# Products of zeros in TensorE's planned gaps before the first tokens, in an attention and two-layer feed-forward kernel

## The chip, the cores and the metric

One Trainium2 chip, one of its cores. The metric is the device time of one execution in microseconds (us), less is better. The engines are TensorE (PE; its weight loads are shown apart as PEld), VectorE (DVE), ScalarE (ACT), GpSimd (POOL) and SyncE (SP), which issues the transfers.

## What is computed

Two attentions over the same q, k, v (4 batches, 8 heads, 576 tokens, 64 per head) are added: one over means of 4 tokens, whose rows are repeated 4 times, and one local, where a token sees those less than 4 places away. The sum goes, as 2304 tokens of 512, through two feed-forward layers.

```python
out_d = sm_attn(q_d, k_d, v_d)            # q_d, k_d, v_d: means over 4 tokens
out_up = np.repeat(out_d, factor, axis=2)
mask = np.abs(pos[:, None] - pos[None, :]) < factor
scores = np.where(mask, scale * np.matmul(q, k.transpose(0, 1, 3, 2)), -1000000000.0)
...
out_local = np.matmul(attn, v)
x = (out_up + out_local)                  # as 2304 x 512
x = ((x @ w_a) * (x @ w_b)) @ w_out       # d_ff 1536
h = x @ w_in                              # d_ff 2048
return (h * np.clip(h + 3.0, 0.0, 6.0) / 6.0) @ w_out2
```

All is float32. The weights arrive as 64-bit numbers and are decoded on the chip.

## The kernel before

The work is cut into steps. Each step is handed to a planner, the class `Plan`, with its engine, the time that it will keep the engine busy, a due time (`want`), the steps that it comes after, and tokens that it takes and gives back (buffers, banks of PSUM, turns). `Plan.run` lets time pass by these costs. Whenever an engine is free, the ready step with the least due time that can have its tokens is begun, and its instructions are written into the program at that moment. So the plan fixes the order of instructions on each engine, once; on the chip each engine runs its instructions in that order and waits for the data of each. The planner's times are in us: 0.07 + 0.00106 n for VectorE over n elements (`dve`), 0.0039 per KB of a transfer plus 2.5 until it has landed, and 0.35, 0.25 and 0.2 from the end of a step of TensorE, ScalarE or VectorE until another engine may use the result.

The 2304 tokens are cut into units of 116 (the last of each batch has 112), and the units into seven blocks: two units in the first, three in the others. The steps that matter here, with their lines:

- `pooled`, once for each batch and pair of heads g: load q and k (L372, 590 KB by the plan's count) and v (L377); sums of 4 tokens on VectorE (L395); scores on TensorE (L405, 2.0 by the plan in the first batch; 32 matrix products of float32 there, 64x72 against 64x144); maximum (L410) and scale (L413) on VectorE; exponentials on ScalarE (L419); normalisation on VectorE (L352); two transposes on TensorE (L437), each followed by a copy on ScalarE (L444); products with v on TensorE (L455); a copy on ScalarE (L461).
- `local`, once for each unit: mask and scores on TensorE (L497, L503); maximum on VectorE (L511); exponentials on ScalarE (L520); normalisation (L352); transposes (L536) and a copy (L540); products with v on TensorE, which in the first batch start from the pooled part (L546, L550); then the tokens x in two float32r parts, the first by ScalarE (L571), the second by VectorE (L574).
- `decode`: each 1024 KB piece of a weight goes through one ScalarE step (L240), eight VectorE instructions (L246 to L271) and one more ScalarE step (L268).
- `job`: for one block and one piece of w_a and w_b, 24 products on TensorE (L609), a copy (L615) and a product (L618). The first job needs the tokens of both units of the first block.

Everything later (L666, the first layer's output; L792 and L915, the second layer by seven products in place of eight) is TensorE's for the most part.

PSUM in this stage has two pairs of banks, token "s2", for scores, and four single banks, token "b", for transposes, for value products and for the jobs' sums. At most one transpose ("turn", 1) and one value product ("pv", 1) hold a bank at a time, and "m" (3) caps the banks that jobs hold. A score of the pooled attention takes a pair that the exponentials give back, so the third score waits for the exponentials of the first.

In the plan the first four scores, those of the four pairs of heads of batch 0, begin at 5.68, 7.98, 10.80 and 16.95 on TensorE.

Of the kernel before, what the change touches and what calls it, by code (L numbers as in the profile page):

```python
# [11 lines left out]
BF16 = mybir.dt.bfloat16  # L12
# [6 lines left out]
P = 128  # L19
# [12 lines left out]
BLOCKS = (2, 3, 3, 3, 3, 3, 3)  # L32
XT = 3 * UT
NC = 512
NB = 384
CUT = 4
BANK = 512
# [19 lines left out]
class Plan:  # L57
# [4 lines left out]

    def __init__(self):
        self.steps, self.cap, self.queue = [], {}, {}
        self.loose = set()

    def add(self, engine, busy, want, run, after=(), take=(), give=(), late=0.0):

        i = len(self.steps)
        self.steps.append((engine, busy, (want, i), run, [a for a in after if a is not None], take, give, late))  # L70
        for tag in take:
            self.queue.setdefault(tag, []).append((want, i))
        return i

    def run(self):
        left = [len(s[4]) for s in self.steps]
        users = [[] for _ in self.steps]
        for i, s in enumerate(self.steps):
            for a in s[4]:
                users[a].append(i)  # L80

        for q in self.queue.values():
            heapq.heapify(q)
        ready, free, events, now, done = {}, {}, [], 0.0, 0
        for i, s in enumerate(self.steps):
            ready.setdefault(s[0], [])
            free[s[0]] = 0.0
            if not left[i]:
                heapq.heappush(ready[s[0]], s[2])

        def can(i):
            return all(self.cap[tag] > 0 and (tag in self.loose or self.queue[tag][0][1] == i)
                       for tag in self.steps[i][5])

        while True:
            moved = True
            while moved:
                moved = False
                for engine, steps in ready.items():
                    if free[engine] > now:  # L100
                        continue
                    for w in sorted(steps):
                        if can(w[1]):
                            break
                    else:
                        continue
                    steps.remove(w)
                    heapq.heapify(steps)
                    i = w[1]
                    _, busy, _, run, _, take, give, late = self.steps[i]  # L110
                    for tag in take:
                        self.cap[tag] -= 1
                        if tag not in self.loose:
                            heapq.heappop(self.queue[tag])
                    run()
                    done += 1
                    moved = True
                    free[engine] = now + busy
                    heapq.heappush(events, (now + busy, -1, i))
                    heapq.heappush(events, (now + busy + late, i, i))  # L120
            if not events:
                break
            now, kind, i = heapq.heappop(events)
            if kind < 0:
                continue
            for tag in self.steps[i][6]:
                self.cap[tag] += 1
            for u in users[i]:
                left[u] -= 1
                if not left[u]:  # L130
                    heapq.heappush(ready[self.steps[u][0]], self.steps[u][2])
        if done != len(self.steps):
            stuck = [(engine, self.steps[i][3].__qualname__.split("fused_kernel")[-1], w, self.steps[i][5], self.cap)
                     for engine, steps in ready.items() for w, i in steps]
            raise RuntimeError(f"{len(self.steps) - done} steps cannot begin, as {stuck[:9]}")
# [3 lines left out]
def fused_kernel(ctx: ExitStack, tc: tile.TileContext, qk, vt, vd, wab, wo, w2i, w2o, mask, out):  # L139
    nc = tc.nc  # L140
# [16 lines left out]
    ap = actx.enter_context(tc.tile_pool(name="attn", bufs=1))  # L157
# [7 lines left out]
    ready = const.tile([P, 1], F32, name="ready")  # L165
# [2 lines left out]
    make_identity(nc, ident)  # L168
    ident16 = ap.tile([P, P], BF16, name="ident16")
    make_identity(nc, ident16)  # L170

    h_d = [dram.tile([P, NT], F32, name=f"h_d{f}") for f in range(F1)]

    plan = Plan()
# [9 lines left out]
    def slot(pool, shape, dtype, tag, name):  # L184
        return pool.tile(shape, dtype, tag=tag, bufs=BUFS[tag], name=name)
# [16 lines left out]
    def PE(busy, want, run, after=(), take=(), give=(), slack=0.0):  # L202
        return plan.add("PE", busy, want, run, after, take, give, PE_L + slack)
# [9 lines left out]
    def DMA(kb, want, run, after=(), take=(), give=()):  # L213
        i = plan.add("SP", dma(kb), want, run, after, take)
        j = plan.add("-", 0, want, lambda: None, [i], give=give, late=DMA_L)
        issued[j] = i
        return j
# [116 lines left out]
    def unit_tokens(u):  # L334
        return min(UT, S - u % NU * UT)

    place, sizes = {}, []
    for m, n in enumerate(BLOCKS):
        sizes.append(0)
        for _ in range(n):  # L340
            u = len(place)
# [6 lines left out]
    S_ = {}  # L348
# [8 lines left out]
    def one_bank(name):  # L357
        return slot(ps, [P, BANK], F32, "b", name)
# [274 lines left out]

    cuts = list(range(0, NT, NC)) + [NT]
    spans = list(zip(cuts, cuts[1:]))
    hs, accs, x2_d = {}, {}, {}

    def hg_slot(f, name):
        return slot(pools["p3" if f % 4 == 3 else "p2"], [P, 2, NC], F32R, f"hg{f % 4 // 3}", name)

# [3 lines left out]
    def second(n, f, want):  # L644
# [45 lines left out]
        for e in range(KC):  # L690
            T = {}

            def out_of(e=e, T=T):
                T["t"] = (slot(pools["p4"], [P, NB], F32, "c", "x2f") if end else
                          slot(pools["p3"], [P, NC], F32, "xo", "x2f"))[:, :nb]
                nc.scalar.activation(T["t"], accs[n][e], AF.Copy)

            def store(e=e, T=T):
                for m in range(lo // NB, (hi - 1) // NB + 1):
                    if m not in x2_d:  # L700
                        x2_d[m] = dram.tile([KC, P, NB], F32, name=f"x2_d{m}")
                    a, b = max(lo, m * NB), min(hi, m * NB + NB)
                    nc.sync.dma_start(x2_d[m][e][:, a - m * NB:b - m * NB], T["t"][:, a - lo:b - lo])

            tag = "c" if end else "xo"
            j = ACT(act(nb), want, out_of, [i, S_["p4"] if end else None], take=[tag], give=["q"])
            j = DMA(nb // 2, want, store, [j], give=[tag])
            for m in range(lo // NB, (hi - 1) // NB + 1):
                S_.setdefault(("x2d", m), []).append(j)
# [270 lines left out]
    for u in place:  # L980
        m = place[u][0]
        i = (place[u][1] + UT - 1) // UT
        t = when[m, 0] - 4 + 0.1 * i if m < 3 else T1 - 30 + 4 * i if m == 3 else T1 - 14 + 1.25 * (i + 3 * m - 12)
        if u % NU == 0:
            for g in range(HP):
                pooled(u // NU, g, t - 0.05 + 0.01 * g, u // NU < 1)
        local(u, t, m < 3 and unit_tokens(u) == UT)
    for f in range(F1):
        S_["wab", f] = decode(wab[f], when[0, f] - 4, lambda f=f: wab_t.setdefault(f, slot(wpool, [P, 2, W], F32R, "wh", "wh")),
                              "wh", ahead=26 if f < 2 else 6, slack=0.0)  # L990
# [118 lines left out]
    for i, (n, h) in enumerate((n, h) for n in ORDER for h in range(2)):  # L1109
# [8 lines left out]
        def second(n=n, h=h):  # L1118
# [4 lines left out]
                take=["wh" if i < F1 else "w2"])  # L1123
        j = ACT(act(W), T4 - 4 + 4 * i, first, [j])
        S_["w2o", n, h] = DVE(dve(W), T4 - 4 + 4 * i, second, [j])
    for p in range(PAIRS):
        outer(p, T4 + 56 * p)
    plan.run()


# [67 lines left out]
```

## Time and profile before

| | us |
|---|---|
| median of 3 runs | 946.65 |
| lowest and highest | 945.78, 947.98 |
| the profiled execution | 948.64 |
| its span, first to last instruction | 946.8 |
| TensorE busy in the span | 927.8 |
| VectorE busy | 756.0 |
| ScalarE busy | 456.3 |

The profile is of one execution. Busy times add up an engine's instructions; a clock of 1.00 means that TensorE is granted its upper level, 2.4 GHz, and 0.50 the lower, 1.2 GHz. Where the profile has no record of the clock (the first stretches) the table shows 1.00. Matrix products overlap: one that takes 294 ns from begin to end can be followed by the next much sooner.

### The profile page before, as it was taken

Reading aid. Unit: us, or ns where it says so; the run is one execution under the profiler, and the core shown is the slowest. Engines: PE = TensorE matmul, PEld = TensorE weight load, DVE = VectorE, ACT = ScalarE, POOL = GpSimd, SP = SyncE. Lnnn points to the kernel's source line nnn. Section 1 sums busy time; section 2 is a strip of 40 time slices with the busy share of each in tenths; the row PEclk is TensorE's granted clock in tenths of the full one; section 3 lists DMA queues with packets and bytes.
Section 4 is the critical chain, followed back from the end, with each engine's and each line's share of the span. In section 5 each row is a group of like instructions: output and inputs, shape, how many; then the busy total and the mean of one; then the engine's idle time right before and its main releaser. Section 6 shows DMA issues by size and latency. Waiting matters only on the chain.

```text
span 946.8 us, 19011 instructions
## 1 busy us (share of the span) xinstructions
PE 927.8 (98%) x7246; PEld 874.9 (92%) x7246; DVE 756.0 (80%) x1375; ACT 456.3 (48%) x1164; POOL 5.4 (1%) x44
## 2 busy tenths in 40 slices
PE   7899999999999999999999999999999999999998
PEld 6678989999989999998888889999999999999998
DVE  4999999924736959686877856999898999897983
ACT  4677455423555424233444435555455574554551
POOL 1000000000000000000000000000000000000000
PEclk9799999999999999999999999999999999999999
DMA  9644563423205444426677887425248871806301
GB/s 272 181 131 151 188 213 136 142 85 117 96 31 158 159 139 142 134 70 201 192 229 249 262 255 234 143 96 189 105 159 266 269 256 53 282 2 212 123 18 52
DMA packets 103726, 151.26 MB, mean 160 GB/s; under 512 B 8785, under 2 KB 72273, under 8 KB 103633
## 3 DMA queue, kind: packets, MB, share of 16 engines
q1 hardware_dynamic: 102944, 148.80, 49.0%
q8 instruction: 57, 0.93, 0.4%
q10 hardware_dynamic: 688, 1.23, 0.4%
q14 instruction: 37, 0.29, 0.1%
HBM read 100.19 MB, written 49.81 MB: 158 GB/s over the span
## 4 chain that ended last, share of the span: by engine, by line
PE 86%; DVE 10%; DMA 1%; issue 1%; ACT 1%; SPq 0%; DVEq 0%; ACTq 0%
PE pab L609 32%; PE ph L792 16%; PE oacc L915 15%; PE acc L666 14%; PE po L550 2%; PE dsc L405 2%; DVE in L722 2%; PE sc L503 1%; PE pt L536 1%; PE dpo L455 1%; DVE w2o L1120 1%; DMA h<-h_d 1%; DVE e L888 1%; DVE part L808 1%; PE po L546 1%
## 5 line engine op out<-in xcount | busy, mean ns | idle before, releaser
L609 PE MATMUL pab<-x,wh 128*128 128x344 f32 (+2 forms) x2016 | 321.3, 318 | 0.1
L609 PEld LDWEIGHTS pab<-x,wh 128*128 128x128 f32 x2016 | 308.0, 189 | 3.6 <-issue 1.9
L915 PE MATMUL oacc<-w2o,in 128*128 128x256 f32 x1512 | 181.9, 283 | 1.4 <-DVE in L722 1.4
L915 PEld LDWEIGHTS oacc<-w2o,in 128*128 128x128 f32 x1512 | 181.3, 192 | 2.0 <-DVE in L722 1.8
L792 PE MATMUL ph<-in,w 128*128 128x384 f32 x1008 | 175.4, 335 | 0.0
L792 PEld LDWEIGHTS ph<-in,w 128*128 128x128 f32 x1008 | 175.2, 188 | 0.0
L666 PE MATMUL acc<-h,wo 128*128 128x512 f32 (+1 forms) x720 | 151.2, 371 | 1.3 <-ACT h L654 0.8
L666 PEld LDWEIGHTS acc<-h,wo 128*128 128x128 f32 x720 | 125.7, 188 | 26.8 <-DVE h L658 1.7
L808 DVE TENSOR_TENSOR part<-ph,part 128x384 f32<-128x384 f32 x168 | 86.1, 554 | 9.3 <-PE ph L792 8.6
L618 DVE TENSOR_TENSOR a<-a,pab 128x344 f32<-128x344 f32 (+2 forms) x84 | 41.4, 494 | 56.3 <-PE pab L609 46.7
L816 ACT ACTIVATE r<-part,three 128x384 f32<-128x384 f32 x96 | 56.4, 613 | 54.9 <-DVE part L808 52.4
L654 ACT ACTIVATE h<-h 128x512 fp32r<-128x512 f32 (+1 forms) x60 | 35.1, 589 | 81.5 <-DMA h<-h_d 63.5
L615 ACT ACTIVATE a<-pab 128x344 f32<-128x344 f32 (+2 forms) x84 | 36.8, 445 | 77.7 <-PE pab L609 53.2
L658 DVE TENSOR_TENSOR h<-h 128x512 fp32r<-128x512 f32 (+1 forms) x60 | 37.9, 636 | 37.4 <-ACT h L654 37.3
L719 ACT ACTIVATE in<-gr 128x384 fp32r<-128x384 f32 x96 | 47.4, 521 | 41.4 <-PE oacc L915 29.0
L240 ACT ACTIVATE m<-raw 128x1024 f32<-128x1024 f32 x34 | 39.3, 1155 | 42.6 <-DVE raw L258 23.4
L722 DVE TENSOR_TENSOR in<-gr,in 128x384 fp32r<-128x384 f32 x96 | 50.2, 563 | 7.0 <-ACT in L719 6.3
L719 ACT ACTIVATE in<-e 128x384 fp32r<-128x384 f32 x72 | 36.5, 526 | 33.9 <-PE oacc L915 21.3
L819 DVE SCALAR_TENSOR_TENSOR r<-r,part 128x384 f32<-128x384 f32 x96 | 50.7, 555 | 1.2 <-ACT r L816 1.1
L520 ACT ACTIVATE e<-sc,mx 128x64 f32<-128x64 f32 x160 | 48.1, 322 | 5.3 <-DVE mx L512 5.3
L258 DVE SCALAR_TENSOR_TENSOR raw<-raw,m 128x1024 f32<-128x1024 uint32 x34 | 41.7, 1227 | 1.2
L251 DVE SCALAR_TENSOR_TENSOR raw<-raw,m 128x1024 uint32<-128x1024 uint32 x34 | 41.5, 1221 | 0.2
(86 smaller groups left out, 899.3 us busy)
## 6 DMA issues: line engine op xcount, KB each, us to landing
g_d<-r SPq DMA_DIRECT2D x96, 192.0 KB, 1.9
gr<-g_d SPq DMA_DIRECT2D x48, 384.0 KB, 4.9
raw<-wab SPq DMA_DIRECT2D x12, 1024.0 KB, 11.2
h<-h_d SPq DMA_DIRECT2D x48, 256.0 KB, 3.1
h_d<-a SPq DMA_DIRECT2D x48, 172.0 KB, 1.9
raw<-w2o SPq DMA_DIRECT2D x32, 256.0 KB, 3.5
qk<-qk SPq DMA_DIRECT2D x14, 576.0 KB, 5.7
w2o<-w_d SPq DMA_DIRECT2D x14, 512.0 KB, 10.1
```

The lines of the kernel that those rows point to most:

```text
L251: nc.vector.scalar_tensor_tensor(out=hi, in0=hi, scalar=0xC0000000, in1=T["m"].bitcast(U32), op0=ALU.bitwise_and, op1=ALU.bitwise_or)
L258: nc.vector.scalar_tensor_tensor(out=lo.bitcast(F32), in0=lo, scalar=2.0 ** -52, in1=m, op0=ALU.mult, op1=ALU.mult)
L520: nc.scalar.activation(L["e"][:, p, h], L["s4"][:, p, h], AF.Exp, bias=L["mx"][:, p, h:h + 1], scale=SCALE, accum_out=L["z"][:, p, h:h + 1])
L609: nc.tensor.matmul(T[k], wab_t[f][:, x, c], xs[n][:, g, y, :nb], start=(g == 0 and i == 0), stop=(g == KC - 1 and i == 2))
L666: nc.tensor.matmul(accs[n][e], wo_t[f // 2][:, x, c], hs[n, f][:, y], start=(f == 0 and i == 0), stop=(f == F1 - 1 and i == 2))
L719: nc.scalar.activation(x[0][:, 0], src(), AF.Copy)
L722: nc.vector.tensor_tensor(x[0][:, 1], src(), x[0][:, 0], op=ALU.subtract)
L792: nc.tensor.matmul(acc[k], t[:, x, g * P:(g + 1) * P], X[k, g][0][:, y], start=(g == 0 and n == 0), stop=(g == 1 and n == 2))
L808: nc.vector.tensor_tensor(s[name], acc[k], s[other], op=ALU.add)
L816: nc.scalar.activation(T["r"], src(), AF.Relu, bias=three)
L819: nc.vector.scalar_tensor_tensor(out=T["r"], in0=T["r"], scalar=6.0, in1=src(), op0=ALU.min, op1=ALU.mult)
L915: nc.tensor.matmul(acc[n][e], X[n, k][0][:, x, e * P:(e + 1) * P], t[:, y], start=(k == 0 and i == 0), stop=(k == K - 1 and i == 2))
```

## The change

The class `Plan` gets a `filler`. When an engine is free and none of its ready steps can begin, and the engine is the filler's, and the time since the last filler is at least 0.4 (`FILL`), the filler is run: it keeps the engine busy for 0.25 in the plan, and two events wake the planner, one at its end and one 0.4 after its beginning. The filler is one product of a 128x128 tile of bf16 zeros with the same tile repeated four times, 512 columns, into a bank that nothing reads. That bank is taken from "b" and counted once in "m" by a first step, due before everything else, which also runs the first such product; a last step, which keeps no engine busy, ends the filling and gives both tokens back when ScalarE has written the first token part of both units of the first block. The zeros are written by one memset on VectorE, behind that of `three`.

```diff
+FILL = 0.4
...
+        self.filler = None
...
-        ready, free, events, now, done = {}, {}, [], 0.0, 0
+        ready, free, events, now, done, fill = {}, {}, [], 0.0, 0, 0.0
...
                     else:
+                        if self.filler and engine == self.filler[0] and now >= fill:
+                            _, busy, period, run = self.filler
+                            run()
+                            free[engine], fill = now + busy, now + period
+                            heapq.heappush(events, (now + busy, -1, -1))
+                            heapq.heappush(events, (fill, -1, -1))
                         continue
...
+    idle = ap.tile([P, P], BF16, name="idle")
+    nc.vector.memset(idle, 0.0)
+    unread = []
+
+    def fill():
+        if not unread:
+            unread.append(one_bank("unread"))
+        nc.tensor.matmul(unread[0], idle, idle.unsqueeze(1).to_broadcast([P, BANK // P, P]), start=True, stop=True)
...
+    def end_fill():
+        plan.filler = None
+
+    i = plan.add("PE", 0.01, -1000, fill, take=["b", "m"])
+    plan.add("-", 0, -1000, end_fill, [i, *(S_["x", u] for u in place if place[u][0] < 1)], give=["b", "m"])
...
+    plan.filler = ("PE", 0.25, FILL, fill)
     plan.run()
```

## Rows read from the trace of the kernel before

**Rows 1.** The page: busy us, share, instructions; granted clock in 40 slices, in tenths.
```profile
PE 927.8 (98%) x7246; PEld 874.9 (92%) x7246; DVE 756.0 (80%) x1375; ACT 456.3 (48%) x1164; POOL 5.4 (1%) x44
...
PEclk9799999999999999999999999999999999999999
```

**Rows 2.** Stretches: begin:end, us, busy of each engine (instructions), clock, DMA share, GB/s.
```profile
12.60:21.27 8.67, 8.51 (x140) 7.66 (x141) 6.18 (x16) 6.42 (x37) 0.00 (x0) 1.00 1.05 272
21.27:39.50 18.23, 14.52 (x230) 11.63 (x229) 17.78 (x30) 13.32 (x55) 0.00 (x0) 0.87 0.78 235
39.50:45.00 5.50, 5.49 (x69) 3.51 (x70) 4.81 (x9) 3.75 (x15) 0.00 (x0) 0.51 0.28 70
45.00:50.80 5.80, 5.67 (x85) 3.79 (x85) 5.51 (x13) 4.89 (x23) 0.00 (x0) 1.00 0.91 276
50.80:66.00 15.20, 14.82 (x204) 12.12 (x203) 14.19 (x33) 8.99 (x38) 0.00 (x0) 1.00 0.35 102
```

**Rows 3.** Waits of VectorE, 21 to 66: us in total, times, longest.
```profile
DVE dmx L410 <- PE dsc L405: 1.4, 1, 1.4
DVE x L574 <- ACT x L571: 0.6, 1, 0.6
DVE a L618 <- PE pab L609: 0.6, 2, 0.3
```

**Rows 4.** Line L405 in 5.5 to 10.5 and 10.8 to 14: ns least/median/most.
```profile
L405 PE MATMUL dsc<-dqk,qk x38: 443/444/524, 5.9 to 10.3; 64*72 64x144 f32 x38
...
L405 PE MATMUL dsc<-dqk,qk x44: 283/294/409, 10.6 to 13.9; 64*72 64x144 f32 x44
```

**Rows 5.** The chain of waits in order of time: start, us, what.
```profile
5.93 4.15 PE dsc L405 x32
```

**Rows 6.** TensorE in order of time, 12 to 16: start, us, line, operation, tiles.
```profile
12.76 2.41 PE L405 MATMUL dsc<-dqk,qk 64*72 64x144 f32 x32 [0.22 <-ACT de L419]
...
15.38 0.39 PE L497 MATMUL sc<-mask_sb,ident 128*128 128x256 bf16 x2
15.70 0.69 PE L503 MATMUL sc<-qk 64*64 64x64 f32 x32
```

**Rows 7.** VectorE in order of time, its first two instructions.
```profile
0.80 0.06 DVE L164 MEMSET three<- 128x1 f32 x1 [0.80 <-PEq L1188]
...
5.12 0.75 DVE L395 TENSOR_REDUCE dqk<-qk 128x144 f32<-128x576 f32 x1 [4.26 <-DMA qk<-qk]
```

**Rows 8.** Groups of instructions on TensorE, 431 to 700: count, busy, mean ns, idle.
```profile
L666 PE MATMUL acc<-h,wo 128*128 128x512 f32 (+1 forms) x720 | 151.2, 371 | 1.3 <-ACT h L654 0.8 <-DVE h L658 0.3
```

**Rows 9.** TensorE in order of time, 39.5 to 47.
```profile
39.51 1.92 PE L546 MATMUL po<-od,ident 128*128 128x464 f32 x2 [0.39 <-ACT od L461]
41.36 1.97 PE L550 MATMUL po<-eT,vz 128*64 128x58 f32 x32
43.26 0.61 PE L497 MATMUL sc<-mask_sb,ident 128*128 128x256 bf16 x2
43.80 1.14 PE L503 MATMUL sc<-qk 64*64 64x64 f32 x32
44.86 1.04 PE L546 MATMUL po<-od,ident 128*128 128x464 f32 x2
45.84 1.15 PE L550 MATMUL po<-eT,vz 128*64 128x58 f32 x32
```

**Rows 10.** One more stretch, with the columns of rows 2.
```profile
123.40:126.80 3.40, 3.40 (x13) 3.40 (x13) 3.33 (x6) 0.32 (x1) 0.00 (x0) 0.50 1.03 374
```

**Rows 11.** TensorE in order of time, just ahead of that stretch.
```profile
122.49 0.72 PE L405 MATMUL dsc<-dqk 64*72 64x144 f32 x8 [1.62 <-DVE dqk L395]
```

**Rows 12.** ScalarE and VectorE in order of time, 42 to 45.
```profile
43.40 0.56 ACT L571 ACTIVATE x<-po 128x464 fp32r<-128x464 f32 x1 [1.75 <-PE po L550]
...
42.15 1.22 DVE L271 TENSOR_TENSOR wh<-raw,wh 128x1024 fp32r<-128x1024 f32 x1
...
43.99 0.64 DVE L574 TENSOR_TENSOR x<-po,x 128x464 fp32r<-128x464 f32 x1 [0.62 <-ACT x L571]
```

## The prediction, made before the changed kernel was run

> **What bounds the kernel now.** I read the page first: TensorE is busy for 98% of the span, and the row of granted clocks has one slice well below full, the second, with the first just under [rows 1]. So nearly all of the time is TensorE's, and the change can only touch the first 50 us. The table by stretches comes next [rows 2]. The reader is to see two things in it. From 21.27 to 39.50 VectorE is busy for 17.78 of 18.23 us while TensorE has 3.7 us idle: there VectorE sets the pace (it decodes the first weights between the attention steps), and a faster TensorE gains nothing. From 39.50 to 45.00 TensorE is busy all the time but at a granted clock of 0.51, the lower level of 1.2 GHz; before it had worked with gaps. From 45.00 on it is at full clock with next to no gaps. The list of VectorE's waits [rows 3] then says where VectorE, the bound from 21.27 on, is held by TensorE: 1.4 us before the fourth pooled maximum (L410, the wait ends at 21.27), and 0.6 us before the first unit's second token part (L574), which ScalarE's copy hands on. These two are the only large doors through which work on TensorE's clock can move the end.
>
> The first stretch needs the durations themselves, as the table has no low clock for it. The score matmuls of L405 take 444 ns (median) up to 10.3 us and 294 ns after [rows 4], and the first 32 take 4.15 us in the chain [rows 5] where the third 32 take 2.41 [rows 6]. So TensorE starts at the lower level, after doing nothing up to 5.93, and rises some 4.8 us after it began.
>
> **The change part by part.**
> *Setup.* One memset on VectorE follows the 0.06 us one at 0.80 [rows 7]; VectorE then waits until 5.12 for keys, so this is hidden, and the products can begin at about 1.0. The added constant tile and the unread bank cost room alone: up to the end of filling the plan has one of "turn" and one of "pv" out at a time, so three banks instead of four and two "m" instead of three hold nothing back. The cover here is those two caps. Without it one reuse would wait for a ScalarE copy.
>
> *How many products.* This follows from the planner's own costs. Its first score waits for 590 x 0.0039 + 2.5 of load and 0.68 + 0.2 of sums, 5.68. So the fill at 0 and 15 more, one each 0.4, go ahead of it: 16. After that the plan of before has 15 gaps on TensorE until the second unit's tokens, 12.7 in all; with one product at the start of each and one each 0.4 on, that is some 38. What counts is where they stand: one between the first two scores, three ahead of the third, one and three between the third and the fourth. The other 30 come after the fourth score. There VectorE is the bound and TensorE has those 3.7 us idle [rows 2]; 19 or so of the 30 lie ahead of 39.5, and 19 x 0.21 is 4.0, just about the idle time, so I cost them at nothing. If that cover is thin, each product that sticks out costs 0.21.
>
> *Price of one.* No product of 128x512 bf16 stands in the trace. The nearest row by shape is L666, 512 columns at one pass: 151.2 us for 720, 0.21 [rows 8]. The other bound is the pair of bf16 mask products of 256 columns, 15.38 to 15.70, 0.32 for the same 512 columns [rows 6]; at the lower clock the pair takes 43.26 to 43.80, 0.54 [rows 9]. I take 0.21, and double it, 0.42, at half clock. The Trainium skill ("TensorE: Matmul & The Clock Gate", Back-to-back issue gap) gives about 131 ns for 512 columns in a stream with weight loads; the eight products among the scores would then cost 0.6 us less than below and the whole would be 0.6 better. Row 151.2 / 720 contradicts it, and I go by the row.
>
> *The start.* The clock rose 4.8 us after work began [rows 4]; 5.4 us after the gaps ended at 39.5 [rows 2]; 3.4 us was the length of another spell at half clock [rows 10]. From 1.0 on this gives a rise at 5.8 (4.4 to 6.4). By 5.8, 11.4 products are done at 0.42, and the other 4.6 take 0.97: the first score begins at 6.8 instead of 5.93. It then takes 2.41, not 4.15, and ends at 9.2 instead of 10.08. One product and the second score follow, to 11.8; the third score could begin 2.68 after the first ends (12.76 less 10.08), 11.9, but three products end at 12.4. It begins 0.3 us earlier than before. Then the four products between third and fourth score lie on a stretch in which TensorE had no gap (8.51 of 8.67 us) and add 0.84. So the fourth score, and with it VectorE's chain, comes **0.5 us later**. Bounds: products done by 5.93, 0.3 earlier; clock never up before they end at 7.7, 1.4 later; at 0.32 a product in the busy part, 0.9 more.
>
> *The cold stretch.* With products in the gaps TensorE should stay at full clock from 34.6 to 44.9. The first unit's value products take 3.8 us from 39.51 to 43.33; the next unit's, at full clock, take 2.13 [rows 9]. So ScalarE's copy, which idled 1.75 us for them, can come 1.8 earlier [rows 12]. But VectorE ends its weight part at 43.37 and began L574 at 43.99 [rows 12]: only **0.6 us** of the 1.8 are worth anything, as the next wait of VectorE is one for the weight products of L618 [rows 3], which TensorE reaches in its turn, behind steps that wait for VectorE. Five products in the plan's gap of 1.76 stand ahead of the second unit's value products, 1.05 us; those come 1.8 + 0.9 earlier at full clock, so this is hidden.
>
> *Sum.* +0.5 - 0.6 = -0.1 us. The profiled execution of 948.64 would become 948.5. That execution lies 2.0 above the median of the runs shown, so against the median the forecast is 946.5.
>
> **The rivals.**
> *The clock comes too late, or the products are dearer* (chance 0.15). The last of the 16 ends at 7.7; +1.4 - 0.6 gives 947.4, and with the dear products up to 948.3. For it: only 7 us lie ahead, and one known rise needed 5.4. Against it: the products come without a gap from 1.0 on, and two of the three known spells were shorter.
> *The change doesn't do what it says* (0.08). The clock falls at 34.6 all the same, since products stand where the plan has gaps, not where the chip has them: then +0.5 stands alone, 947.1.
> *A better order by accident* (0.18). Each product delays a ready step in the plan by up to 0.25, so all that is planned after is sorted anew. At 122.49 TensorE waits 1.62 us for a sum on VectorE and then runs 3.4 us at half clock [rows 10, 11], which loses 1.7: 3.3 us together. If the new order puts that sum ahead, the time is 946.5 - 3.3 = 943.2. For it: VectorE is ahead of TensorE by little there. Against it: the same plan costs hold, so the same mistake is likely to stay.
> *Slower: one such stall more* (0.12). The same mechanism the other way: another step that is queued on TensorE ahead of a sum which VectorE reaches 1.6 us late, in the 50 us after the filling, where VectorE is busy for 14.19 of 15.20 us [rows 2]. It costs 1.6 and another 1.7 of half clock: 949.8. It decides from a wait of about 2 us on.
> The forecast itself has 0.47.
>
> **How the numbers follow.** A measurement of this kernel tells 0.2% from no change, 1.9 us. The forecast and the first two rivals lie within that, but for their tails: same 0.63. Faster: the better order and 0.05 of the forecast's tail, where the first score begins at 5.93 and VectorE's order lets more of the 1.8 us through (-0.9 to -2.1): 0.23. Slower: one stall more and 0.02 of tail: 0.14. The forecast alone spans 944.5 to 948.3. Reaching into both order cases until 2 in 10 are out, the range is 943.8 to 948.9.
>
> **What would show it.** In the changed profile there should be about 54 products of 128x512, the first 16 from about 1.0 to 6.8. The first 32 scores should take 2.4 us, beginning at 6.1 to 7.7. VectorE's wait before the fourth maximum should grow and that step begin at 20.9 to 22.7. The clock should be full in 34.6 to 44.9, and the wait of L574 be gone. The first weight products (L609) should begin within 1 us of where they did. I would be wrong if the clock fell again, if products ahead of 39.5 held VectorE up, or if the time differs though the first 66 us end alike: then it is the order.

## The result: slower by half a per cent

| | us |
|---|---|
| kernel before, median | 946.65 (945.78 to 948.05) |
| changed kernel, median | 952.2 (950.42 to 953.58) |
| ratio | 1.0051, 95% interval 1.0040 to 1.0062 |
| profiled execution of the changed kernel, and its span | 952.62, 950.8 |

The two medians alone give a ratio of 1.0059, inside the interval. The forecast was 946.5 with a range up to 948.9, so the result lies outside, on the side that had a chance of 0.14.

The products themselves did what they were to do. The page of the changed kernel first: busy us, share and instructions of each engine, and the granted clock in 40 slices.

```profile
PE 935.8 (98%) x7299; PEld 875.2 (92%) x7299; DVE 755.5 (79%) x1376; ACT 458.0 (48%) x1164; POOL 5.2 (1%) x44
...
PEclk9999999999999999999999999999999999999999
```

No slice is at 7 any more [rows 1]. There are 53 more instructions, the products, and TensorE is busy for 8.0 us more. By the rows below the products take some 14 (5.98 for the first 16, 0.22 for each of the others), so by this estimate its other work takes some 6 us less; the first score alone gives 1.7 of them (4.15 before [rows 5], 2.41 now). Next its first steps in order of time (start, us, line, operation, tiles, count):

```profile
1.02 5.98 PE L188 MATMUL unread<-idle 128*128 128x512 bf16 x16 [1.02 <-DVE idle L182]
6.93 2.41 PE L423 MATMUL dsc<-dqk,qk 64*72 64x144 f32 x32
...
15.04 0.39 PE L188 MATMUL unread<-idle 128*128 128x512 bf16 x1
15.27 0.41 PE L455 MATMUL dpt<-ident,de 72*72 72x72 f32 x4
15.61 2.42 PE L423 MATMUL dsc<-dqk,qk 64*72 64x144 f32 x32
...
42.97 1.25 PE L188 MATMUL unread<-idle 128*128 128x512 bf16 x5
44.06 0.94 PE L564 MATMUL po<-od,ident 128*128 128x464 f32 x2
...
50.62 1.58 PE L627 MATMUL pab<-x,wh 128*128 128x232 f32 x12
```

(L423 is L405 of before, L455 L437, L564 L546, L627 L609.) There are 16 products ahead, from 1.02, and the first score begins at 6.93 and takes 2.41. Five products take 1.09 from 42.97 to 44.06, 0.22 each. So far the working holds to 0.2 us. But the fourth score is at 15.61, ahead of the first unit's scores; in the kernel before, those came first, at 15.38 [rows 6]. TensorE's order has changed at its fifth step of the plan. The first weight products begin at 50.62, as early as in the kernel before:

```profile
50.76 2.50 PE L609 MATMUL pab<-x,wh 128*128 128x232 f32 x20
```

So the loss shows only behind them. Two tables show where. First the waits of TensorE between 50 and 145 us (us in total, times, longest), then two stretches with the columns of rows 2:

```profile
PE po L568 <- ACT eT L558: 2.6, 2, 1.9
PE pab L627 <- ACT a L633: 1.1, 2, 0.8
PE dpo L473 <- ACT deT L462: 1.0, 1, 1.0
PE pt L554 <- DVE e L370: 0.7, 1, 0.7
PE pab L627 <- DVE wh L289: 0.7, 1, 0.7
PE dpt L455 <- DVE de L370: 0.5, 1, 0.5
```

```profile
66.00:145.00 79.00, 73.66 (x772) 66.57 (x769) 74.19 (x117) 44.65 (x145) 0.64 (x8) 0.98 0.56 175
...
77.50:80.90 3.40, 3.29 (x18) 2.83 (x18) 3.33 (x6) 1.43 (x8) 0.00 (x0) 0.50 0.64 217
```

TensorE waits 6.6 us there. The same table of the kernel before has three rows:

```profile
PE dsc L405 <- DVE dqk L395: 1.6, 1, 1.6
PE sc L497 <- ACT de L419: 0.3, 1, 0.3
PE po L550 <- ACT eT L540: 0.2, 1, 0.2
```

That is 2.1 us. In the 79 us from 66 on TensorE was busy for 77.22 there, 3.6 us more than now:

```profile
66.00:145.00 79.00, 77.22 (x816) 71.08 (x817) 74.71 (x119) 44.90 (x151) 0.82 (x8) 0.98 0.55 173
```

The half-clock spell of 3.4 us that stood at 123.4 [rows 10] now stands at 77.5, behind waits of 0.97 and 0.65. So TensorE waits for other engines' steps that stand too late, in another order, and 4.5 us of added waiting is about the added time of the two profiled spans, 4.0. That the order is the cause is for the experiments to show.

### The profile page after: what moved, and what is told of

The parts are those of the page before. It is cut to its first block, busy times and chain, and to the rows that moved or that the text cites. A ratio compares the mean times of both kernels' runs of the same rounds, so it can differ in the third digit from the quotient of the medians.

```text
span 950.8 us, 19126 instructions
## 1 busy us (share of the span) xinstructions
PE 935.8 (98%) x7299; PEld 875.2 (92%) x7299; DVE 755.5 (79%) x1376; ACT 458.0 (48%) x1164; POOL 5.2 (1%) x44
## 4 chain that ended last, share of the span: by engine, by line
PE 82%; DVE 9%; DMA 7%; issue 1%; ACT 1%; ACTq 0%; DVEq 0%
PE pab L627 29%; PE ph L810 18%; PE oacc L933 16%; PE acc L684 14%; DMA raw<-wab 4%; DMA qk<-qk 2%; PE po L568 1%; DVE in L740 1%; PE sc L521 1%; DVE wh L289 1%; PE pt L554 1%; DVE raw L276 1%; DMA h<-h_d 1%; DVE e L906 1%; DVE raw L282 1%
## 5 line engine op out<-in xcount | busy, mean ns | idle before, releaser
L627 PE MATMUL pab<-x,wh 128*128 128x344 f32 (+2 forms) x2016 | 323.1, 318 | 1.8 <-ACT a L633 1.1
L627 PEld LDWEIGHTS pab<-x,wh 128*128 128x128 f32 x2016 | 307.5, 189 | 6.2 <-issue 2.3
L737 ACT ACTIVATE in<-e 128x384 fp32r<-128x384 f32 x72 | 36.4, 525 | 33.3 <-PE oacc L933 19.7
```

The costliest lines, as they stand in the source:

```text
L627: nc.tensor.matmul(T[k], wab_t[f][:, x, c], xs[n][:, g, y, :nb], start=(g == 0 and i == 0), stop=(g == KC - 1 and i == 2))
L737: nc.scalar.activation(x[0][:, 0], src(), AF.Copy)
```

## The experiments

Ratios are to the kernel before, measured on the same chip (median 947.4 in each of the three sets).

### The order of before with the products, and the order of after without

`e1_order_before`: a product costs the plan nothing, so every engine has the order of the kernel before, with 58 products in it.

```diff
-                            free[engine], fill = now + busy, now + period
-                            heapq.heappush(events, (now + busy, -1, -1))
+                            fill = now + period
...
-    i = plan.add("PE", 0.01, -1000, fill, take=["b", "m"])
+    i = plan.add("PE", 0.0, -1000, fill, take=["b", "m"])
```

> The products are issued at the planner's gaps as in the changed kernel, but keep TensorE busy for nothing in the plan, so every engine has the order of steps of the kernel before (16 products ahead of the first score, 42 between steps). Theory A, the order planned behind the filling costs the 5 us and the products nothing: 946.0 us (945.0 to 947.5), no step behind the filling waits longer than before. Theory B, the products hold up the steps they stand in front of: 950 us or more, with the first weight products 3 us later than before.

Measured: 946.22 us, ratio 0.9989 (0.9980 to 0.9998), as theory A has it. Its waits of TensorE from 50 to 145:

```profile
PE dsc L422 <- DVE dqk L412: 1.3, 1, 1.3
PE sc L514 <- ACT de L436: 0.3, 1, 0.3
```

`e2_order_after`: the changed plan with its filler, but `fill` issues nothing.

```diff
     def fill():
-        if not unread:
-            unread.append(one_bank("unread"))
-        nc.tensor.matmul(unread[0], idle, idle.unsqueeze(1).to_broadcast([P, BANK // P, P]), start=True, stop=True)
+        pass
```

> The plan of the changed kernel with its filler, but no product is issued: the order of steps of the changed kernel and TensorE idle in the gaps. Theory A: slower than before by as much as the changed kernel, 952 us (950.5 to 954), with the waits of TensorE at 76 and 122 us. Theory B: as the kernel before, 946.7 us (945.5 to 948.5).

Measured: 956.42 us, ratio 1.0100 (1.0082 to 1.0118). Its waits in the same stretch, and its first weight products:

```profile
PE po L566 <- ACT eT L556: 1.7, 2, 1.0
PE pt L552 <- DVE e L368: 1.3, 1, 1.3
PE dpo L471 <- ACT deT L460: 1.0, 1, 1.0
PE pab L625 <- ACT a L631: 0.8, 2, 0.5
PE pab L625 <- DVE wh L287: 0.6, 1, 0.6
PE dpt L453 <- DVE de L368: 0.5, 1, 0.5
```

```profile
55.22 1.58 PE L625 MATMUL pab<-x,wh 128*128 128x232 f32 x12
```

This pair settles that the order is what costs. The same six kinds of wait stand in the changed kernel and in its order without products, and none of those six stands in the order of before with products. The order costs 1.00% by itself, 9 us; with about the same products, the two orders are 0.62% apart (0.9989 and 1.0051), 6 us. Theory A was too low for e2: in that order the products are worth some 4.6 us (the first weight products begin at 55.22 without them and 50.62 with them), and without them TensorE is granted 0.50 from 34.6 to 44.9 there, while VectorE is busy for only 6.92 of the 10.30 us (9.51 in the kernel before), so that in that order VectorE does not hide a slow TensorE. The changed kernel is a loss of 9 us with 4 to 5 of it paid back.

### Which products help, in the order of before

`e3_ahead` has only the 16 ahead of the first score, `e4_between` only the 42 behind it: in e1's line that asks for a filler, `and now < 5.68` and `and now >= 5.68` are added; in e4 the first step issues nothing.

> The order of the kernel before, and only the 16 products ahead of the first score. Theory A: the first score at full clock, 2.4 us long and ended 0.8 us earlier, the fourth maximum on VectorE 0.7 us earlier than 21.27; the clock falls again at about 35 us as before; 945.9 us (945.0 to 947.0). Theory B: the products ahead delay the first score by 1 us and this stays: 947.5 us.

Measured: 945.5 us, ratio 0.9983 (0.9975 to 0.9992), as theory A has it.

> The order of the kernel before, and only the 42 products in the gaps behind the first score. Theory A: first 32 scores 4.1 us as before, the fourth maximum 0.5 to 0.9 us later than 21.27, clock full from 34 to 45 us, which gives back 0.6: 946.8 us (945.8 to 948.0). Theory B: 950 us or more.

Measured: 948.18 us, ratio 1.0008 (0.9999 to 1.0017): just above the range of theory A, far from B, and no clear change. The first score on TensorE, in e3 (with the second), e4 and e1 in this order:

```profile
6.01 4.55 PE L422 MATMUL dsc<-dqk,qk 64*72 64x144 f32 x64
...
6.15 4.13 PE L422 MATMUL dsc<-dqk,qk 64*72 64x144 f32 x32 [6.15 <-DVE dqk L412]
...
6.70 2.42 PE L422 MATMUL dsc<-dqk,qk 64*72 64x144 f32 x32
```

The fourth maximum on VectorE, in the same three:

```profile
19.64 0.75 DVE L427 TENSOR_REDUCE dmx<-dsc 72x4 f32<-72x576 f32 x1 [1.30 <-PE dsc L422]
...
23.34 0.75 DVE L427 TENSOR_REDUCE dmx<-dsc 72x4 f32<-72x576 f32 x1 [2.00 <-PE dsc L422]
...
22.05 0.75 DVE L427 TENSOR_REDUCE dmx<-dsc 72x4 f32<-72x576 f32 x1 [2.00 <-PE dsc L422]
```

and the stretch 34.6 to 44.9 in e3 and then in e4 (columns of rows 2):

```profile
34.60:44.90 10.30, 9.91 (x132) 6.82 (x128) 9.44 (x18) 7.97 (x37) 0.00 (x0) 0.68 0.45 139
...
34.60:44.90 10.30, 9.97 (x137) 6.49 (x134) 10.13 (x16) 7.71 (x36) 0.00 (x0) 1.00 0.37 124
```

The step stood at 21.27 in the kernel before [rows 2]. The products ahead bring it 1.6 forward. Those between the steps put it back 2.1 when alone, and e1 is 2.4 behind e3. Not all of this is their price, as the first score does not begin at the same time. From its begin to the fourth maximum it is 13.6 us in e3, 15.35 in e1, 17.2 in e4 and 15.3 in the kernel before (5.93 to 21.27), so the nine products that stand there cost 1.7 (e1 against e3) to 1.9 (e4 against before); the other 0.7 between e1 and e3 come from the 16 products ahead, which took 5.75 us in one execution and 4.94 in the other. In return the clock stays full. Both signs are as expected, and both sizes are more than twice what I wrote.

### Taking the order apart by splicing

`e5_late_before` follows the changed kernel, products too, up to the end of the filling, and takes the steps that are left in the order of before. `e6_late_after` has no products and follows the order of before up to that point, then that of after. For both, `Plan.run` makes the two orders without issuing, and issues one list; a step is taken when those that it comes after are issued and its tokens are free.

```diff
+        first = first[:first.index(end) + 1]
+        done = {i for i in first if i >= 0}
+        then = [i for i in (a if THEN == "after" else b) if i >= 0 and i not in done]
```

> The changed kernel, products and order, up to the end of the filling; from there each engine takes the steps that are left in the order of the kernel before (nine of some 3600 had to go ahead of it). Theory A1, the whole loss of the changed kernel lies in the order behind the filling: 946.5 us (945.5 to 948), the waits at 76, 122 and 129 us gone. Theory A2, the order within the first 45 us costs too: 949 us or more.

Measured: 960.98 us, ratio 1.0149 (1.0135 to 1.0163).

> No products; the order of the kernel before up to the first block's tokens, then the steps that are left in the order of the changed kernel. Theory A1: the loss of the changed kernel without the products' gain, 951.8 us (950.5 to 953.5). Theory A2: 948.5 us or less.

Measured: 958.43 us, ratio 1.0111 (1.0097 to 1.0124). Neither fits theory A1 or A2. Waits of TensorE from 45 to 145, e5 and then e6:

```profile
PE dsc L471 <- ACT de L485: 6.8, 3, 2.7
PE pt L602 <- DVE e L418: 2.0, 1, 2.0
```

```profile
PE sc L563 <- ACT e L586: 2.4, 1, 2.4
PE po L616 <- ACT eT L606: 2.0, 2, 1.3
PE dpo L521 <- ACT deT L510: 1.0, 1, 1.0
PE pab L675 <- ACT a L681: 0.8, 2, 0.6
PE pab L675 <- DVE wh L337: 0.6, 1, 0.6
PE dpt L503 <- DVE de L418: 0.5, 1, 0.5
```

A splice has waits of its own (6.8 and 2.0 in e5, 2.4 in e6), since the second half was planned for another first half. So e5 is inconclusive: whether the early order costs by itself stays open. e6 still says one thing: its five other rows are of kinds that e2 has, with an early order that is that of before. Those 4.9 us of waiting come with the late order, whichever early order stands ahead of it.

### Other orders from the same planner

If the plan decides, any change of its two numbers gives another order, better or worse. Three kernels change them alone (`FILL`, and the 0.25 of a product).

```diff
-FILL = 0.4
+FILL = 0.5
...
-    plan.filler = ("PE", 0.25, FILL, fill)
+    plan.filler = ("PE", 0.15, FILL, fill)
```

> The changed kernel with two other numbers in the plan alone: a product counts 0.15 instead of 0.25 and comes every 0.5 instead of 0.4 (49 products instead of 52 behind the first; TensorE's order of steps the same as before for the first 22). The plan ends 6.3 earlier than that of the kernel before, where the changed kernel's ends 3.2 later. If the order decides and the plan foresees it: 941 us (939 to 945). If the order decides and the plan does not foresee: anywhere from 944 to 955. If the products decide: 952 us as the changed kernel.

> The same with 0.15 and every 1.0 (28 products): the plan ends 4.3 later than that of the kernel before. If the order decides and the plan foresees it: 952 us (949 to 955). If products decide, fewer of them cost less: 949 us. If the order decides and the plan does not foresee: anywhere from 944 to 955.

> The changed kernel with 0.18 in the plan for a product and one every 0.5: the plan ends 3.2 earlier than that of the kernel before and has 4.9 of idle time on TensorE from 46 to 200 (kernel before 5.2, changed kernel 9.7, 0.15 and 0.5: 2.3). If the time follows the idle time of the plan in that stretch, it is that of the order of the kernel before with products, 946.2 us (945 to 947.5). If it follows the plan's end, 944 us. If the plan tells nothing, anywhere from 944 to 955.

| | plan: idle on TensorE, 46 to 200 | plan's end against before | measured us | ratio |
|---|---|---|---|---|
| e7, 0.15 and 0.5 | 2.3 | -6.3 | 945.57 | 0.9982 (0.9973 to 0.9991) |
| e1, order of before | 5.2 | 0 | 946.22 | 0.9989 (0.9980 to 0.9998) |
| e12, 0.18 and 0.5 | 4.9 | -3.2 | 948.98 | 1.0016 (1.0007 to 1.0025) |
| after, 0.25 and 0.4 | 9.7 | +3.2 | 952.2 | 1.0051 (1.0040 to 1.0062) |
| e8, 0.15 and 1.0 | 9.8 | +4.3 | 953.69 | 1.0064 (1.0047 to 1.0082) |

The plan's idle time is counted to some 0.3. With products in all five, the times spread over 8 us and do not follow the number of products (29, 50, 52, 53 and 58 in e8, e7, e12, after and e1). In e8 a part of the loss can be the clock, as its few products leave 0.83 from 34.6 to 44.9; the four others have 1.00 there. The plan's own idle time behind the filling tells the two bad orders from the three others, and so do TensorE's waits in the traces from 50 to 145 us: 4.7 in e8 and 6.6 in after, 0.3 in e7, 1.6 in e1, none listed in e12. Among those three neither ranks. Of the forecasts, that from the plan's end failed for e7 and e12, and e12 came out 2.8 above what it was expected to equal by its idle time. A part of that goes with the clock: its seven executions with a mean granted clock of 0.997 or 0.998 took 948.98 to 950.20, the four at 0.999 or 1.000 took 947.15 to 948.91. The rest stays open.

`e11_015_none` is e7's order with no product issued, as in e2.

> The plan with 0.15 and 0.5, its order, and no product issued. The order alone against that of the kernel before, both without products. If the gain of 1.8 us lies in the order: 945.6 us. If the order is worth nothing and the products gave it: 947.4 us. If the order is the worse one and only the products, which keep the clock, made it good (as they gave back some 4 us of the changed kernel's loss): 949 us or more.

Measured: 946.5 us, ratio 0.9987 (0.9979 to 0.9996). By the medians the order is 0.9 us better than that of before and the products add 0.9 to it; by the ratios it is 1.2 and 0.5, and the intervals of e7 and e11 overlap. So the products are worth 1 us or less in both good orders, and over 4 only in the bad one.

### Leaving out the products that stand in the way

`e9_before_skip` is e1 and `e10_015_skip` is e7, each without the products between the first and the fourth score (each score of the pooled attention adds itself to `scored`).

```diff
+    scored = []
+
     def fill():
+        if 0 < len(scored) < 4:
+            return
```

> The order of the kernel before with the products, but the nine between the first and the fourth score left out. If those stand on the path to VectorE's chain and the later ones are hidden, as the working of the prediction has it: the fourth maximum at 19.7 us, as with the 16 ahead alone, the clock full from 5.4 on, and 944.7 us (943.8 to 945.6), 0.8 below the 16 ahead alone and 1.5 below all products in this order. If the later ones cost what they give: 945.5 us.

Measured: 946.6 us, ratio 0.9994 (0.9985 to 1.0002). The first score with the second, and the fourth maximum:

```profile
7.44 4.55 PE L427 MATMUL dsc<-dqk,qk 64*72 64x144 f32 x64
...
21.07 0.75 DVE L432 TENSOR_REDUCE dmx<-dsc 72x4 f32<-72x576 f32 x1 [1.35 <-PE dsc L427]
```

From the one to the other it is 13.6 us as in e3, so the nine products cost their 1.7 there. But the maximum is only 1.0 ahead of e1 and not at the 19.7 of the expectation, as the 16 products took 6.49 in this execution. The first weight products begin at 49.61 against 50.59 in e1. This does not show in the time, whose interval overlaps that of e1. In 390 to 600, TensorE's waits on the tokens between the layers, e9 and then e1:

```profile
PE acc L688 <- ACT h L676: 1.7, 2, 1.4
PE acc L688 <- DVE h L680: 0.9, 1, 0.9
PE pab L631 <- ACT a L637: 0.6, 1, 0.6
```

```profile
PE acc L683 <- DVE h L675: 0.7, 2, 0.5
PE acc L683 <- ACT h L671: 0.4, 1, 0.4
```

That is 3.2 against 1.1 in one execution each; whether the earlier start causes it was not tried.

> The plan with 0.15 and 0.5, its order and products, but the six between the first and the fourth score left out. Theory: 1.2 us of product time leaves the path to the fourth maximum, 944.3 us (943.3 to 945.3). If the first scores are bound by the loads in this order: 945.6 us, as with them.

Measured: 944.39 us, ratio 0.9970 (0.9958 to 0.9981), as forecast. It beats both kernels, by 3 us the kernel before. The path is shorter as the theory has it: from the begin of the first score to the fourth maximum it is 13.6 us against 14.7 in e7 (6.42 to 20.06, 5.92 to 20.64). That the 1.2 us below e7 come from this is not shown: the two intervals overlap, and the same cut gained nothing in e9. From 50 to 145 TensorE waits once, as in e7:

```profile
PE pab L632 <- DVE wh L293: 0.3, 1, 0.3
```

## Why the prediction was wrong

*The start* was right as a mechanism. The first score at 6.8 was forecast, 6.93 came; 2.41 for it; 0.21 a product against 0.22. That the 0.21 came so near was luck: the 720 products of its row [rows 8] are of two shapes, and those of 512 columns alone take 133.0 for 576, 0.23:

```profile
L666 PE MATMUL acc<-h,wo 128*128 128x512 f32 x576 | 133.0, 392 | 0.3 <-DVE h L658 0.3
```

The fourth maximum was to come 0.5 late. In the kernel where it can be compared, e1, it came 0.8 late (22.05). The count of eight products among the scores missed one: in the order of before there are nine, five of them between the third and the fourth score, and one product is 0.2 of the 0.3. In the changed kernel the maximum is at 18.08, by the new order, and tells nothing.

*The cold stretch* was right in kind: the clock is full from 34.6 to 44.9 and VectorE's wait for the first unit's second token part is gone in e1. (The value products come 1.7 earlier by the rows, not 1.8; only 0.6 was counted.) The first weight products begin at 50.59 there, 0.2 earlier than the 50.76 of before, although the fourth maximum is 0.8 late, so 1.0 came back where I had 0.6. The sum of -0.1 was -0.2 there, and the time of e1 is 1.1 below its kernel before. The other 0.9 stay open. The half-clock spell at 123.4 [rows 10], which I put at 1.7 and which e1's profiled execution does not have, would cover them, but in how many executions of the kernel before it stands is not known.

*The step that failed* is the one in which I counted the products and then went on with the order of before: "What counts is where they stand". A product keeps TensorE for 0.25 in the plan, and I took what this does to the order ("sorted anew") only as a pair of rivals, 0.18 on the fast side and 0.12 on the slow side, each worth one stall. The very first gaps show why that was too little. In the plan of before the pooled normalisation and the fourth pair's sums compete for VectorE at about 11.7. The normalisation is ready at 11.69 there and goes first; the data of the sums are there at 11.70. The products put the first score back from 5.68 to 5.86, so the normalisation is ready 0.13 later, the sums go first, and the fourth score takes TensorE at 13.71 for 2.0, where the first unit's scores had stood at 13.10. A lead of 0.01 us decides it, and the later steps follow from it. None of the four settings tried (after, e7, e8, e12) keeps the order of before. What the runs showed in place of the step: the order by itself costs 1.00%, 9 us (e2), and with products in both orders that of before is 6 us ahead (e1). The last sign that the prediction named is the one that came: its first weight products begin where they did, and the time differs.

*The size* was off too. The slow rival asked for one wait more, 1.6, for a sum on VectorE in the 50 us behind the filling, and for 1.7 of half clock. What came was 4.5 us more of waiting, in six kinds of wait, and the spell moved to another place rather than one more. 4.7 of the 6.6 us are waits for ScalarE, and 3.7 of them stand at 122 us and later, so the rival was right in kind, a step that TensorE reaches too early, and only in part in its place. Its price of 3.3 is about half of what the order cost: against e1 the waits are 6.6 to 1.6, and the spell of 3.4 us at 0.50 is lost as well, which gives 5.0 + 1.7 where the two profiled spans are 6.0 apart.

*The other rivals:* the clock came in time, and it did not fall in the gaps that were filled. A better order by accident did not come in the changed kernel, but it is possible: that of e7, without products, is better than that of before (e11, ratio 0.9987, 0.9979 to 0.9996).

## What to carry to other kernels

When a list scheduler writes the order, anything that takes time in its plan can change the whole plan behind it, and the price of that is not bounded by the price of what was added: here products of 0.25 in the plan, which gain 1 us in the order of before, made an order that costs 9 without them and 5 with them. Put filler work in after the order is made, or at no cost in the plan, and compare orders before costing instructions. The idle time that the plan itself leaves on the engine that bounds the kernel is worth a look beforehand, as it told the two bad orders of five; the one forecast made from it, for e12, failed. And filler belongs where the engine waits by the trace: the products ahead of the first work brought VectorE's chain forward, while the nine between steps that had no gap put it back by 1.7 to 1.9 us.

## What the hardware showed that I had not expected

The same 16 products ahead of the first score took 5.98 us in the changed kernel, 5.75 in e1, 4.94 in e3 and 6.49 in e9, one execution each. A single one lasts 634 ns at first and 380 later, so the clock rises at a different moment of the same work from one execution to the next; a filler sized to end with the loads will sometimes overrun them.

Keeping TensorE at the upper level in its lowest stretch gained no time that these runs show where VectorE is the bound. From 34.6 to 44.9 e3 is granted 0.68 and e1 1.00, with VectorE busy for 10.13 of 10.30 us, and e1 is not faster (946.22 against 945.5); how much of that is the time of its products and how much the clock was not taken apart. The times of the kernel before agree: in the 73 executions of the kernel before that were taken with the experiments, the median is 947.4 for those with a mean granted clock of 0.992 or less and 947.6 for those of 0.995 or more. In the six executions of e2, the changed order without products, clock and time go together: 954.12 us at 0.995, 960.14 at 0.985.
